# Routing attention and a PReLU feed-forward block on one core: cluster masks on two row tiles, denominators on four column tiles, two weight conversions a step, and v loaded apart from q and k

## The chip, the core and the metric

The kernel runs on one core of one Trainium2 chip. Its metric is the device time of the whole program in microseconds (us). The core's engines are named as in the profile: PE is the matrix engine (PEld its weight loads), DVE the vector engine, ACT the scalar engine, POOL the gpsimd engine, SP the engine whose queue issues nearly all DMAs. Each engine takes its instructions in program order; they wait for one another through semaphores.

## The reference, cut to what matters

```python
# q, k, v: (4, 8, 768, 64); centroids: (8, 16, 64)
q_n, k_n, c_n = (a / (norm(a) + 1e-06) for a in (q, k, centroids))
q_assign = argmax(einsum('bhsd,hcd->bhsc', q_n, c_n), -1)     # the cluster of each query
k_assign = argmax(einsum('bhsd,hcd->bhsc', k_n, c_n), -1)     # the cluster of each key
mask   = q_assign[:, :, :, None] == k_assign[:, :, None, :]
scores = where(mask, q @ k.T / sqrt(64), -1e9)
attn   = exp(scores - max(scores)); attn /= attn.sum(-1) + 1e-09
x      = (attn @ v), heads side by side: (3072, 512)
# w_in: (512, 2048), w_out: (2048, 512), alpha: (2048,), in float64
h = x @ w_in
out = (maximum(h, 0) + alpha * minimum(h, 0)) @ w_out
```

A query attends only to keys of its own cluster. The feed-forward weights arrive as 64-bit floats and are turned into 32-bit ones on the chip.

## The kernel before, in words

**Units of work.** A pair `n` is one batch and two heads: 16 pairs, of which `n < NCH` (0 to 3) are batch 0. The 768 queries of a pair are done in two halves of `HS` = 384. The 768 keys are six chunks of 128, numbered 0 to 5. Scores are held transposed, 128 keys by 384 queries. The order is batch, half, pair; one (batch, half) is a block, and after each block its 384 rows go through the feed-forward part (FFN), in pieces that are fed between the attention steps of the next block: `hidden(f)` (16 of them, one 128-row slice of `h` each, line 614 and its activations) and `final` (lines 634 to 642).

**Steps.** Up to `TOGETHER` (step 24) a step `u` does two chunks (`GROUP`), so a (pair, half) takes three steps. Steps 0 to 11 are block 0 (batch 0, first half, no FFN yet), steps 12 to 23 block 1 (batch 0, second half, with the FFN of block 0). Three or four steps before step 0 load and prepare. From step 24 on a (pair, half) does all six chunks at its first step. In a step the program issues: `score` of this step's chunks; `weigh` of the chunks of the step before; the bookkeeping on DVE; then three slots, each with FFN pieces, preparation of later pairs and weight conversions. `tick()` releases work that was put off by some slots with `later`.

**`score`** does the score matmuls of two chunks (line 461). For batch 0 (`early_mask`) the cluster mask is added in PSUM by four more matmuls per step (line 471): 32 rows of the tile `member` (one-hot clusters of the keys) against 32 rows of `aq` (one-hot clusters of the queries). The keys' one-hot rows of chunk `c` lie in row group `g = (6 + c) // 3`: chunks 0, 1, 2 in rows 64 to 95, chunks 3, 4, 5 in rows 96 to 127. A step takes chunks (0,1), (2,3) or (4,5). ACT then writes `E = exp` (line 482). `prep_queries` fills `aq` one step ahead, for batch 0 by two DVE copies per (pair, half) (line 421). For later batches DVE masks `E` itself (line 495).

**`weigh`** multiplies `E` with `v` into the one PSUM tile `pos` (line 570). In block 0 it also makes the softmax denominators on PE: ones against `E`, 64 output columns for each head (line 565), into `first_den`. When all six chunks are in, DVE transposes `first_den`, takes reciprocals, transposes back to `rd` (lines 576 to 584), and `normalise` (line 591) writes `xT` and frees `pos`. From step 12 on the denominators are sums on DVE: `add_up` (line 508), `turn` (514), `rows_sums` (520), and then `total`, a matmul on PE (line 530), and `invert` (lines 540 to 547). From step 24 on the masks, sums, `total` and `invert` stand in a list `todo`, one entry a slot.

**Preparation.** For pairs of batch 0 `prep_features` transposes q and k on PE in three groups (line 311) into two PSUM buffers in turn, and ACT moves each group to `qkT` (line 315), so the third group waits for the first move. Then comes `square` on ACT (line 323), which frees the raw q and k tiles; `prep_sims` (line 348) and `prep_argmax` (lines 356 to 381) make `member` on DVE. Four pairs of raw tiles would need eight buffers; there are four, so loads wait for `square` of the pair two before.

**Weight conversions.** There are 32, each of 128 x 512 weights. `convert` issues a 512 KB DMA into one of five `raw` tiles (line 230) and at once DVE's `split` (lines 235, 237), which waits for it; four slots later `scale` on ACT (lines 241, 243); two slots later `join` on DVE (lines 247, 250) and on POOL (line 253). In block 0 a step starts one conversion, every fourth step two; in block 1 one and two by turns. The FFN of block 0 needs them in order: `hidden(12)` the first 28, the last `final` all 32. `convert_up_to` forces whatever is missing.

**Loads.** `load(n)` issues on SP's queue the q and k DMAs (line 114; for later batches eight with 128-byte runs, line 119) and then one of v into `vt` (line 125). There are four `vt` buffers, so the v of pair 4 waits until `weigh` has read that of pair 0 for the last time.

```python
        if half == 0:
            load_at.setdefault(max(u - (7 if n < NCH else 9), -AHEAD), []).append(n)
...
        converting = 0 if u < 0 else 1 + (u % 4 == 3) if u < UB else 1 + u % 2
```

Of the kernel before, what the change touches and what calls it, by code (L numbers as in the profile page):

```python
# [14 lines left out]
ALU = mybir.AluOpType  # L15
AX = mybir.AxisListType
PS = bass.MemoryType.PSUM
P = 128
# [3 lines left out]
def kernel(  # L22
# [82 lines left out]
    def load(n):  # L105


        b, hp = pairs[n]
        for w, src in enumerate((q, k)):
            raw = inp.tile([P, NJ, 2, D], FP32, name="qk")  # L110
            for h in range(2):
                rows = src[b, 2 * hp + h]
                if n < NCH:
                    nc.sync.dma_start(out=raw[:, :, h, :],
                                      in_=rows.rearrange("(j p) d -> p j d", p=P))
                    continue
                for x in range(D // Q):
                    r = h * D + x * Q
                    nc.sync.dma_start(
                        out=raw.rearrange("p j h d -> p (j h d)")[r:r + Q, :].rearrange(  # L120
                            "p (t i) -> p t i", i=Q),
                        in_=rows[:, x * Q:(x + 1) * Q].rearrange("(t p) i -> p t i", p=Q))
            raw_qk[n, w] = raw
        vt = vpool.tile([P, 2, NJ, D], FP32, name="vt")
        nc.sync.dma_start(
            out=vt.rearrange("p h j d -> p (h j) d"),
            in_=v[b, 2 * hp:2 * hp + 2].rearrange("h (j p) d -> p (h j) d", p=P))
        vts[n] = vt
# [5 lines left out]
    load(0)  # L134
    load(1)


    ident = const.tile([P, P], FP32, name="ident")
# [291 lines left out]
    assert NJ % GROUP == 0  # L430
# [16 lines left out]
    def score(n, half, chunks, alone=None):  # L447


        qkT = qkTs[n]  # L450
        pss = [[ps_f.tile([P, 512], FP32, name="fps") for h in range(2)] if c == alone else
               ps_s.tile([P, 2, 512], FP32, name="sps") for c in chunks]
        early_mask = n < NCH

        def bank(ps, h):
            return (ps[h] if isinstance(ps, list) else ps[:, h, :])[:, 0:HS]

        for c, ps in zip(chunks, pss):
            for h in range(2):
                r = h * D  # L460
                nc.tensor.matmul(  # L461
                    out=bank(ps, h),
                    lhsT=qkT[r:r + D, S + c * P:S + (c + 1) * P],
                    rhs=qkT[r:r + D, half * HS:(half + 1) * HS], start=True,
                    stop=not early_mask)
        if early_mask:
            for c, ps in zip(chunks, pss):
                g, i = divmod(NJ + c, GT)
                r = slice(g * Q, (g + 1) * Q)
                for h in range(2):  # L470
                    nc.tensor.matmul(  # L471
                        out=bank(ps, h), lhsT=members[n][r, h, i * P:(i + 1) * P],
                        rhs=aqs[n, half][r, 0, :], start=False, stop=True)
        for c, ps in zip(chunks, pss):
            E = e_tiles[0]
            e_tiles.append(e_tiles.pop(0))
            if c == alone:
                for h in range(2):
                    nc.scalar.activation(out=E[:, h, :], in_=ps[h][:, 0:HS], func=AF.Exp,  # L479
                                         scale=SCALE)  # L480
            else:
                nc.scalar.activation(out=E, in_=ps[:, :, 0:HS], func=AF.Exp, scale=SCALE)  # L482
            waiting.append((n, half, c, E))

    def last(m):

        return waiting[len(waiting) - m:]
# [12 lines left out]
    def add_up(chunk, former):  # L500

        n, half, c, E = chunk
        if c == 0:
            return
        if c == 1:
            accs[n, half] = accp.tile([P, 2, HS], FP32, name="acc")
        acc = accs[n, half]
        nc.vector.tensor_tensor(out=acc, in0=former[3] if c == 1 else acc, in1=E,  # L508
                                op=ALU.add)

    def turn(n, half):
# [40 lines left out]
    def weigh(m, denominators=False):  # L552


        first = waiting[:m]
        del waiting[:m]
        n, half, c0, _ = first[0]
        if c0 == 0:
            pos[n, half] = ps_v.tile([P, 512], FP32, name="vps")
        po = pos[n, half]  # L560
        if denominators:
            for _, _, c, e in first:
                for h in range(2):
                    r = h * D
                    nc.tensor.matmul(out=first_den[r:r + D, 0:HS], lhsT=ones,  # L565
                                     rhs=e[:, h, :], start=(c == 0), stop=(c == NJ - 1))
        for _, _, c, e in first:
            for h in range(2):
                r = h * D
                nc.tensor.matmul(out=po[r:r + D, 0:HS], lhsT=vts[n][:, h, c, :],  # L570
                                 rhs=e[:, h, :], start=(c == 0), stop=(c == NJ - 1))
        if denominators and c0 + m == NJ:
# [7 lines left out]
            i = 2 * n + half  # L580
            nc.vector.tensor_reduce(out=lowest[:, i:i + 1], in_=denT[:, :, 0],
                                    axis=AX.X, op=ALU.min)
# [88 lines left out]
    for (n, half), u in start_of.items():  # L671
        def at(step, slot, piece):
            prep_at.setdefault((step, slot), []).append(piece)
        if half == 0:
            load_at.setdefault(max(u - (7 if n < NCH else 9), -AHEAD), []).append(n)
            if n < NCH:
                for g in range(len(groups)):
                    at(u - 4, FIRST + g, lambda n=n, g=g: prep_features(n, g))
# [22 lines left out]
        ffn.extend(ffn_pieces(pairs[n][0], half))  # L701

    for u in range(-AHEAD, TOGETHER):
        for n in load_at.get(u, []):
            if n > 1:
                load(n)
# [14 lines left out]
        if ended:  # L721
            normalise(*prior[:2])
        if u >= UB:
            add_up(last(1)[0], last(2)[0]) if s == 0 else [
                add_up(chunk, None) for chunk in last(GROUP)]
            if s == SB - 1:
                turn(n, half)
                rows_sums(n, half)
# [17 lines left out]
    more_room()  # L746
    todo = deque()
    for u in range(TOGETHER, NS + 1):
        for n in load_at.get(u, []):
            load(n)  # L750
        if u < NS:
            n, half, s = steps[u]
        if s == 0 or u == NS:
# [22 lines left out]
            for c in range(1, NJ):  # L776
                todo.append(lambda c=c, E=E: add_up(E[c], E[c - 1]))
# [7 lines left out]
        for i in slots:  # L785
# [185 lines left out]
```

## Time and profile before

| | |
|---|---|
| Time before | 1036.49 us, median of 4 runs (1035.48 to 1038.55) |
| The profiled execution | 1038.5 us, its span on the core 1036.6 us |
| Busy share of the span | PE 97%, PEld 48%, DVE 65%, ACT 33%, POOL 5% |
| Chain that ended last, by engine | PE 86%, DVE 8%, ACT 2%, DMA 2% |
| Block 0 (step 0 to step 12) | 12.9 to 76.9 us |
| Block 1 (step 12 to step 24) | 76.9 to 215.9 us |
| From step 24 | 215.9 to 1036.6 us |

Times are counted from the start of the span. A record of a 32-bit float matmul on PE is half of one instruction, and the records of different tiles of the array can run side by side; the durations that the profile gives for PE's records overlap, so the text counts from the start of one group to the start of the next. The granted clock (PEclk) is the share of the full PE clock that the throttle let through. The share of busy time is a mean over blocks with different limits, so the blocks are read apart.

### The profile page before, as it was taken

Reading aid. Unit: us, or ns where it says so; the run is one execution under the profiler, and the core shown is the slowest. Engines: PE = TensorE matmul, PEld = TensorE weight load, DVE = VectorE, ACT = ScalarE, POOL = GpSimd, SP = SyncE. Lnnn points to the kernel's source line nnn. Section 1 sums busy time; section 2 is a strip of 40 time slices with the busy share of each in tenths; the row PEclk is TensorE's granted clock in tenths of the full one; section 3 lists DMA queues with packets and bytes.
Section 4 is the critical chain, followed back from the end, with each engine's and each line's share of the span. In section 5 each row is a group of like instructions: output and inputs, shape, how many; then the busy total and the mean of one; then the engine's idle time right before and its main releaser. Section 6 shows DMA issues by size and latency. Waiting matters only on the chain.

```text
span 1036.6 us, 10221 instructions
## 1 busy us (share of the span) xinstructions
PE 1008.4 (97%) x3827; PEld 493.9 (48%) x3827; DVE 673.9 (65%) x1155; ACT 345.5 (33%) x676; POOL 55.7 (5%) x71
## 2 busy tenths in 40 slices
PE   8999999779999999999999999999999999999997
PEld 4444444334454454545455454545445454544553
DVE  4896798767666566868756676768757675663111
ACT  5664444423132233314333142323323141321220
POOL 1332222210000000000000000000000000000000
PEclk9999999989999999999999999999999999999999
DMA  9543543130000230213000212313000000000000
GB/s 220 175 136 71 140 118 63 52 66 10 1 1 11 51 46 19 28 35 57 1 1 0 62 21 26 46 31 62 1 0 1 31 1 0 1 11 20 1 1 33
DMA packets 120936, 42.72 MB, mean 41 GB/s; under 512 B 113696, under 2 KB 113712, under 8 KB 120880
## 3 DMA queue, kind: packets, MB, share of 16 engines
q1 hardware_dynamic: 120704, 41.95, 18.5%
q8 instruction: 32, 0.52, 0.2%
q14 instruction: 24, 0.20, 0.1%
q10 hardware_dynamic: 176, 0.04, 0.0%
HBM read 35.69 MB, written 6.29 MB: 41 GB/s over the span
## 4 chain that ended last, share of the span: by engine, by line
PE 86%; DVE 8%; ACT 2%; DMA 2%; issue 1%; SPq 1%; POOL 1%; DVEq 0%; POOLq 0%; ACTq 0%
PE fps L634 31%; PE fps L614 28%; PE vps L570 11%; PE sps L461 9%; PE fps L461 4%; DVE acc L508 2%; PE sps L471 1%; PE fps L565 1%; PE mps L348 1%; DVE gT L606 1%; DVE acc L514 1%; DMA raw<-in_moe_w_in_dram 1%; DVE qkT L330 1%; DVE part L520 1%; DMA raw<-in_moe_w_out_dram 1%
## 5 line engine op out<-in xcount | busy, mean ns | idle before, releaser
L614 PE MATMUL fps<-xT,w_in_sb 128*128 128x384 f32 x1024 | 343.2, 492 | 3.4 <-POOL w_in_sb L253 3.4
L634 PE MATMUL fps<-w_out_sb,gT 128*128 128x512 f32 x768 | 337.1, 595 | 7.2 <-POOL w_out_sb L253 7.0
L614 PEld LDWEIGHTS fps<-xT,w_in_sb 128*128 128x128 f32 x1024 | 192.0, 191 | 147.9 <-issue 7.0
L634 PEld LDWEIGHTS fps<-w_out_sb,gT 128*128 128x128 f32 x768 | 144.7, 190 | 184.9 <-issue 165.9
L606 DVE SCALAR_TENSOR_TENSOR gT<-neg,alpha_neg,gT 128x384 f32<-128x384 f32 x128 | 86.4, 677 | 156.1 <-ACT neg L622 155.5
L621 ACT ACTIVATE gT<-fps 128x384 f32<-128x384 f32 x128 | 62.9, 491 | 276.1 <-PE fps L614 276.1
L461 PE MATMUL sps<-qkT 64*128 64x384 f32 x576 | 112.4, 509 | 0.0
L495 DVE SCALAR_TENSOR_TENSOR raw<-aq,key,raw 128x384 f32<-128x384 bf16 x160 | 88.6, 613 | 15.5 <-ACT raw L482 9.8
L482 ACT ACTIVATE E<-sps 128x768 f32<-128x768 f32 x88 | 67.2, 813 | 72.7 <-PE sps L471 46.3
L570 PE MATMUL vps<-E,vt 128*64 128x384 f32 x448 | 81.6, 491 | 0.0
L495 DVE SCALAR_TENSOR_TENSOR E<-aq,key,E 128x384 f32<-128x384 bf16 x128 | 70.9, 612 | 10.3 <-ACT E L482 6.8
L461 PEld LDWEIGHTS sps<-qkT 64*128 64x128 f32 x576 | 52.6, 190 | 41.2 <-issue 9.9
L508 DVE TENSOR_TENSOR acc<-acc,E 128x768 f32<-128x768 f32 x64 | 61.5, 960 | 15.5 <-ACT E L482 13.3
L642 DVE TENSOR_TENSOR y<-y,fps 128x512 f32<-128x512 f32 x30 | 20.6, 685 | 67.5 <-PE fps L634 67.5
L482 ACT ACTIVATE raw<-sps 128x768 f32<-128x768 f32 x56 | 43.0, 814 | 60.4 <-PE sps L461 60.0
L622 ACT ACTIVATE neg<-fps 128x384 f32<-128x384 f32 x128 | 62.0, 484 | 0.6 <-DVE gT L606 0.6
L640 ACT COPY y<-fps 128x512 f32<-128x512 f32 x24 | 14.1, 586 | 131.9 <-PE fps L634 131.9
L570 PE MATMUL vps<-raw,vt 128*64 128x384 f32 x320 | 56.5, 491 | 0.0
L570 PEld LDWEIGHTS vps<-E,vt 128*64 128x64 f32 x448 | 30.5, 137 | 41.9 <-issue 41.4
L508 DVE TENSOR_TENSOR acc<-acc,raw 128x768 f32<-128x768 f32 x48 | 45.9, 956 | 1.2
L461 PE MATMUL fps<-qkT 64*128 64x384 f32 x192 | 42.1, 516 | 0.0
L479 ACT ACTIVATE raw<-fps 128x384 f32<-128x384 f32 x48 | 21.0, 492 | 48.5 <-PE fps L461 48.5
(100 smaller groups left out, 655.8 us busy)
## 6 DMA issues: line engine op xcount, KB each, us to landing
raw<-in_moe_w_in_dram SPq DMA_DIRECT2D x16, 512.0 KB, 4.7
raw<-in_moe_w_out_dram SPq DMA_DIRECT2D x16, 512.0 KB, 6.0
vt<-in_v_dram SPq DMA_DIRECT2D x16, 384.0 KB, 4.4
out_dram<-y SPq DMA_DIRECT2D x24, 256.0 KB, 2.0
qk<-in_q_dram SPq DMA_DIRECT2D x48, 96.0 KB, 3.9
qk<-in_k_dram SPq DMA_DIRECT2D x48, 96.0 KB, 3.7
qk<-in_q_dram SPq DMA_DIRECT2D x8, 192.0 KB, 4.8
qk<-in_k_dram SPq DMA_DIRECT2D x8, 192.0 KB, 4.5
```

Source lines behind the costliest of these rows:

```text
L461: nc.tensor.matmul(out=bank(ps, h), lhsT=qkT[r:r + D, S + c * P:S + (c + 1) * P], rhs=qkT[r:r + D, half * HS:(half + 1) * HS], start=True, ...
L479: nc.scalar.activation(out=E[:, h, :], in_=ps[h][:, 0:HS], func=AF.Exp, scale=SCALE)
L482: nc.scalar.activation(out=E, in_=ps[:, :, 0:HS], func=AF.Exp, scale=SCALE)
L495: nc.vector.scalar_tensor_tensor(out=E[:, h, :], in0=aqs[n, half][:, h, :], scalar=keys[n][:, NJ + c, h:h + 1], in1=E[:, h, :], op0=ALU.is ...
L508: nc.vector.tensor_tensor(out=acc, in0=former[3] if c == 1 else acc, in1=E, op=ALU.add)
L570: nc.tensor.matmul(out=po[r:r + D, 0:HS], lhsT=vts[n][:, h, c, :], rhs=e[:, h, :], start=(c == 0), stop=(c == NJ - 1))
L606: nc.vector.scalar_tensor_tensor(out=gs[f], in0=neg, scalar=alpha_neg[:, f:f + 1], in1=gs[f], op0=ALU.mult, op1=ALU.add)
L614: nc.tensor.matmul(out=ps[:, 0:HS], lhsT=w_in_sb[:, c, f * P:(f + 1) * P], rhs=xT[:, c, :], start=(c == 0), stop=(c == NCH - 1))
L621: nc.scalar.activation(out=gs[f], in_=ps[:, 0:HS], func=AF.Relu)
L622: nc.scalar.activation(out=neg, in_=ps[:, 0:HS], func=AF.Relu, scale=-1.0)
L634: nc.tensor.matmul(out=ps[:, 0:DM], lhsT=gs[f][:, i * P:(i + 1) * P], rhs=w_out_sb[:, f, :], start=on and f == f0, stop=off and f == f0 + ...
L642: nc.vector.tensor_tensor(out=ys[i], in0=ys[i], in1=ps[:, 0:DM], op=ALU.add)
```

## The change

It has five parts. The chunks of a step become (0,3), (1,4), (2,5), and the mask matmuls go head by head over the two chunks, so that two that follow each other use different row groups. The denominators are made on four column tiles of 32, each with half of the queries (192), so eight matmuls of half the length stand where four stood; DVE's transposition of `first_den` is half as long, and four small reciprocals and two small copies stand where one reciprocal stood. The copies that fill `aq` for batch 0 go from DVE to ACT. In block 1 every step starts two conversions. For later batches v is issued two steps after q and k. In the list from step 24 on, `turn` and `rows_sums` share one slot, an empty entry stands ahead of `total`, and each slot's entry is issued ahead of its FFN pieces. `add_up` takes the first two chunks of a (pair, half) in whatever order they come.

```diff
+    def load_v(n):
+        b, hp = pairs[n]
         vt = vpool.tile([P, 2, NJ, D], FP32, name="vt")
         nc.sync.dma_start(
...
                 for g in range(NG // 2, NG):
-                    nc.vector.tensor_copy(out=aqs[n, half][g * Q:(g + 1) * Q, 0, :],
-                                          in_=members[n][r, 0, :])
+                    nc.scalar.copy(aqs[n, half][g * Q:(g + 1) * Q, 0, :],
+                                   members[n][r, 0, :])
...
         if early_mask:
-            for c, ps in zip(chunks, pss):
-                g, i = divmod(NJ + c, GT)
-                r = slice(g * Q, (g + 1) * Q)
-                for h in range(2):
+            for h in range(2):
+                for c, ps in zip(chunks, pss):
+                    g, i = divmod(NJ + c, GT)
+                    r = slice(g * Q, (g + 1) * Q)
                     nc.tensor.matmul(
                         out=bank(ps, h), lhsT=members[n][r, h, i * P:(i + 1) * P],
                         rhs=aqs[n, half][r, 0, :], start=False, stop=True)
...
             for _, _, c, e in first:
                 for h in range(2):
-                    r = h * D
-                    nc.tensor.matmul(out=first_den[r:r + D, 0:HS], lhsT=ones,
-                                     rhs=e[:, h, :], start=(c == 0), stop=(c == NJ - 1))
+                    for x in range(2):
+                        r = h * D + x * Q
+                        nc.tensor.matmul(out=first_den[r:r + Q, 0:HS // 2],
+                                         lhsT=ones[:, 0:Q],
+                                         rhs=e[:, h, x * HS // 2:(x + 1) * HS // 2],
+                                         start=(c == 0), stop=(c == NJ - 1))
...
-            nc.vector.transpose(out=denT.rearrange("p x i -> p (x i)"),
-                                in_=first_den[:, 0:HS])
+            nc.vector.transpose(
+                out=denT[:, 0:NX // 2, :].rearrange("p x i -> p (x i)"),
+                in_=first_den[:, 0:HS // 2])
...
             inv = rdp.tile([P, 2 * NX], FP32, name="inv")
-            nc.vector.reciprocal(out=inv[:, 0:NX], in_=denT[:, :, 0])
+            for g in range(P // Q):
+                h, x = divmod(g, 2)
+                nc.vector.reciprocal(
+                    out=inv[h * D:h * D + Q, x * NX // 2:(x + 1) * NX // 2],
+                    in_=denT[g * Q:(g + 1) * Q, 0:NX // 2, 0])
+            for h in range(2):
+                nc.vector.tensor_copy(out=inv[h * D + Q:(h + 1) * D, 0:NX],
+                                      in_=inv[h * D:h * D + Q, 0:NX])
...
-            load_at.setdefault(max(u - (7 if n < NCH else 9), -AHEAD), []).append(n)
+            if n < NCH:
+                load_at.setdefault(max(u - 7, -AHEAD), []).append(
+                    lambda n=n: n < 2 or (load(n), load_v(n)))
+            else:
+                load_at.setdefault(u - 9, []).append(lambda n=n: load(n))
+                load_at.setdefault(u - 7, []).append(lambda n=n: load_v(n))
...
-            score(n, half, range(s * GROUP, (s + 1) * GROUP))
+            score(n, half, range(s, NJ, SB))
...
-        converting = 0 if u < 0 else 1 + (u % 4 == 3) if u < UB else 1 + u % 2
+        converting = 0 if u < 0 else 1 + (u % 4 == 3) if u < UB else 2
...
-            todo.append(lambda n=n, half=half: turn(n, half))
-            todo.append(lambda n=n, half=half: rows_sums(n, half))
+            todo.append(lambda n=n, half=half: (turn(n, half), rows_sums(n, half)))
+            todo.append(lambda: None)
             todo.append(lambda n=n, half=half: total(n, half))
...
+            todo.popleft()()
             feed(max(pieces, 0))
             if (s, i) == (SB - 1, SLOTS - 1) and unfinished[0]:
                 feed(1)
             if s > 0:
                 prepare(u, i)
-            todo.popleft()()
```

More of the change, by code (lines that the diff above doesn't have):

```diff
@@ L133 @@
     nc.scalar.dma_start(out=alf, in_=moe_alpha.rearrange("(f p) -> f p", p=P))
-    load(0)
-    load(1)
+    for n in range(2):
+        load(n)
+        load_v(n)
     ident = const.tile([P, P], FP32, name="ident")
@@ L429 @@
     SB = NJ // GROUP
-    assert NJ % GROUP == 0
+    assert NJ == GROUP * SB and SB == GT
     steps = [(b * NCH + hp, half, s)
@@ L498, in mask, with add_up @@
                 in1=E[:, h, :], op0=ALU.is_equal, op1=ALU.mult)
-    def add_up(chunk, former):
+    def add_up(chunk, first=None):
         n, half, c, E = chunk
-        if c == 0:
-            return
-        if c == 1:
+        if first is not None:
             accs[n, half] = accp.tile([P, 2, HS], FP32, name="acc")
         acc = accs[n, half]
-        nc.vector.tensor_tensor(out=acc, in0=former[3] if c == 1 else acc, in1=E,
+        nc.vector.tensor_tensor(out=acc, in0=acc if first is None else first[3], in1=E,
                                 op=ALU.add)
@@ L556, in weigh @@
         del waiting[:m]
-        n, half, c0, _ = first[0]
-        if c0 == 0:
+        n, half = first[0][:2]
+        done = first[-1][2] == NJ - 1
+        if (n, half) not in pos:
             pos[n, half] = ps_v.tile([P, 512], FP32, name="vps")
@@ L571, in weigh @@
                                  rhs=e[:, h, :], start=(c == 0), stop=(c == NJ - 1))
-        if denominators and c0 + m == NJ:
+        if denominators and done:
             denT = asg.tile([P, NX, Q], FP32, name="simT")
-            nc.vector.transpose(out=denT.rearrange("p x i -> p (x i)"),
-                                in_=first_den[:, 0:HS])
-            inv = rdp.tile([P, 2 * NX], FP32, name="inv")
-            nc.vector.reciprocal(out=inv[:, 0:NX], in_=denT[:, :, 0])
-            i = 2 * n + half
-            nc.vector.tensor_reduce(out=lowest[:, i:i + 1], in_=denT[:, :, 0],
-                                    axis=AX.X, op=ALU.min)
+            nc.vector.transpose(
+                out=denT[:, 0:NX // 2, :].rearrange("p x i -> p (x i)"),
+                in_=first_den[:, 0:HS // 2])
+            i = 2 * n + half
+            nc.vector.tensor_reduce(out=lowest[:, i:i + 1], in_=denT[:, 0:NX // 2, 0],
+                                    axis=AX.X, op=ALU.min)
+            inv = rdp.tile([P, 2 * NX], FP32, name="inv")
+            for g in range(P // Q):
[6 more added lines that the diff above has]
+                                      in_=inv[h * D:h * D + Q, 0:NX])
             rd = rdp.tile([P, HS], FP32, name="rd")
@@ L703 @@
     for u in range(-AHEAD, TOGETHER):
-        for n in load_at.get(u, []):
-            if n > 1:
-                load(n)
+        for piece in load_at.get(u, []):
+            piece()
         n, half, s = steps[max(u, 0)]
@@ L723 @@
         if u >= UB:
-            add_up(last(1)[0], last(2)[0]) if s == 0 else [
-                add_up(chunk, None) for chunk in last(GROUP)]
+            if s == 0:
+                add_up(last(1)[0], last(2)[0])
+            else:
+                for chunk in last(GROUP):
+                    add_up(chunk)
             if s == SB - 1:
@@ L748 @@
     for u in range(TOGETHER, NS + 1):
-        for n in load_at.get(u, []):
-            load(n)
+        for piece in load_at.get(u, []):
+            piece()
         if u < NS:
@@ L775 @@
                 todo.append(lambda c=c, E=E: mask(E[c]))
-            for c in range(1, NJ):
-                todo.append(lambda c=c, E=E: add_up(E[c], E[c - 1]))
-            todo.append(lambda n=n, half=half: turn(n, half))
-            todo.append(lambda n=n, half=half: rows_sums(n, half))
+            todo.append(lambda E=E: add_up(E[1], E[0]))
+            for c in range(2, NJ):
+                todo.append(lambda c=c, E=E: add_up(E[c]))
+            todo.append(lambda n=n, half=half: (turn(n, half), rows_sums(n, half)))
+            todo.append(lambda: None)
             todo.append(lambda n=n, half=half: total(n, half))
```

## The prediction

> **What bounds the kernel now.** I read the windows by block first, because the page's 97% for PE is a mean.
>
> ```profile
> 12.90:46.88 33.98, 31.45 (x193) 13.76 (x193) 27.00 (x56) 22.60 (x39) 6.55 (x5) 1.00 0.77 205
> 46.88:76.86 29.98, 29.98 (x177) 12.04 (x176) 28.34 (x54) 19.19 (x31) 12.27 (x8) 1.00 0.46 140
> 76.86:139.31 62.45, 62.26 (x239) 28.96 (x237) 47.20 (x73) 28.06 (x49) 14.81 (x9) 1.00 0.43 93
> 182.56:215.92 33.36, 22.94 (x82) 10.27 (x81) 25.10 (x41) 11.27 (x21) 8.43 (x5) 0.86 0.07 27
> 215.92:251.50 35.58, 33.50 (x113) 16.94 (x112) 26.15 (x47) 10.81 (x23) 0.00 (x0) 0.89 0.29 56
> 251.50:947.00 695.50, 692.38 (x2578) 342.66 (x2578) 467.26 (x784) 211.03 (x429) 0.00 (x0) 1.00 0.11 21
> ```
>
> The columns are the stretch, PE, PEld, DVE, ACT, POOL, the granted clock, DMA share and GB/s. From 251 us to 947 PE has nothing to give back but 3.1 us. The loss is at 182 to 251 us: PE idle for 12.5 us and throttled besides. In the second half of block 0 DVE is as full (28.34 of 29.98) as PE, which will matter. Next, who ended PE's waits, from the waits of PE:
>
> ```profile
> PE fps L634 <- POOL w_out_sb L253: 7.0, 2, 3.6
> PE mps L530 <- DVE part L520: 5.2, 7, 2.1
> PE fps L614 <- POOL w_in_sb L253: 3.4, 1, 3.4
> PE fps L311 <- ACT qkT L315: 1.6, 3, 1.1
> ```
>
> So three waits of 10.4 us for the last converted weights, and seven for `total`. Behind the weights, from the waits of DVE and then of SP's queue:
>
> ```profile
> DVE power L235 <- DMA raw<-in_moe_w_in_dram: 12.0, 4, 5.1
> DVE power L235 <- DMA raw<-in_moe_w_out_dram: 4.1, 1, 4.1
> ```
>
> ```profile
> SPq L125 <- PE vps L570: 203.8, 11, 27.2
> ```
>
> The v load holds SP's queue until `weigh` frees its buffer, the weight DMAs queue behind it, and DVE stands still for them: 5.1, 1.0 and 4.1 us of these waits are in block 1.
>
> What the waits cost beyond themselves, from the windows over the throttled stretches:
>
> ```profile
> 186.23:189.64 3.41, 3.41 (x10) 1.18 (x9) 2.25 (x6) 0.87 (x2) 0.00 (x0) 0.50 0.03 7
> 210.12:220.36 10.24, 6.70 (x18) 3.34 (x20) 5.96 (x14) 1.82 (x3) 1.26 (x1) 0.50 0.29 60
> 247.67:251.08 3.41, 3.41 (x7) 1.67 (x5) 2.59 (x8) 0.00 (x0) 0.00 (x0) 0.50 0.00 0
> ```
>
> Each follows a wait of 2.1 to 3.6 us; each halves the clock (0.50).
>
> **Masks.** From the timeline of PE in block 0:
>
> ```profile
> 63.76 0.82 PE L471 MATMUL sps<-aq,member 32*128 32x384 bf16 x4
> 64.51 1.51 PE L565 MATMUL fps<-E,ones 128*64 128x384 f32 x8
> 65.85 1.46 PE L570 MATMUL vps<-E,vt 128*64 128x384 f32 x8
> 67.24 1.56 PE L461 MATMUL sps<-qkT 64*128 64x384 f32 x8
> 68.73 0.50 PE L471 MATMUL sps<-aq,member 32*128 32x384 bf16 x4
> 69.16 1.51 PE L565 MATMUL fps<-E,ones 128*64 128x384 f32 x8
> ```
>
> Start to start, the four masks take 0.75 us for chunks (4,5), (0,1) alike, one row group, and 0.43 for (2,3), which straddles two groups. After the change all do: 16 steps x 0.32 = 5.1 us of PE, 2.6 in each block.
>
> **Denominators.** Now 1.34 us a step (64.51 to 65.85). The new form, sixteen records of 192 columns on four column tiles, is not in the trace; nearest is the `prep_sims` group (line 348), eight records of 384 columns on four tiles, which with its switches of tile shape takes 0.78 (16.42 to 17.20). Same columns, so 0.78 to 0.85, taken 0.80: 12 steps x 0.54 = 6.5 us. Ends: 0 gained if the tiles go in pairs, 7.7 if the four rounds take the 0.16 each that half of a 0.32 round gives with nothing else. The new shape may add a switch a step; the row for one is line 570, four rounds that start 0.32 apart in a slot of 1.39 (65.85 to 67.24), so 0.11, and twelve more would lose 1.3 us. [...]
>
> DVE's end of a half (lines 576 to 584) took 1.5 us; half a transposition less (0.3), five small operations more (0.12 to 0.15 each, rows of lines 579 and 581) makes 2.0.
>
> **Block 0 does not get this 9.1 us (6.5 + 2.6).** The `aq` copies now stand in ACT's queue, ahead of the moves of the next pair's features (line 315).
> At the start: those moves began at 11.12 us; now they wait behind two copies that wait for `member`'s transposition (line 378, done 14.51). No such ACT copy is in the trace; 0.24 (line 397, 96 columns) and 0.47 (line 315, 512 columns, start to start) bound it, taken 0.39. So the first move starts at 15.3, PE's third group at 16.0 instead of 12.37, and PE idles 3.6 us, as long as the waits that halved the clock. Step 0's mask no longer waits 1.2. Step 1 starts at 19.2 to 20.7 instead of 17.20. Behind it on ACT is `square` of pair 1, which frees the tiles for which SP's queue waits (18.56), and behind that the weight DMA issued at 23.76, which ended DVE's wait at 30.78. I put that landing 2.2 us later (1.5 to 3.5).
> From there DVE had work without a gap to 49.86, with ACT behind it:
>
> ```profile
> 42.00 0.72 ACT L241 ACTIVATE power<-power,low_exp 128x512 uint32<-128x512 uint32 x1 [2.77 <-DVE power L235]
> 45.66 0.58 ACT L315 COPY qkT<-fps 128x512 f32<-128x512 f32 x1
> ```
>
> 42.00 becomes 44.7 (2.2, and 0.5 for DVE's longer end). The move comes 3.66 later plus 0.78 of copies: 49.1. Step 6 starts at 50.3, not 46.88: 3.4 late. PE will have idled some 5 us before it, at half clock after (1.7).
> Steps 6 to 12: step 6 saves 0.86. Then PE's 30.0 us between the ends of the denominators in steps 6 and 12 shrink by 6 x 0.54 + 4 x 0.32 to 25.5, but DVE's 17.2 us without a gap (50.68 to 67.91) shrink only to 16.2 (1.5 of copies at 62.20 off, 0.5 on) where PE wants 13.1. DVE ends 3.1 late, `normalise` frees `pos` 1.8 late for step 10. So 27.3.
> Sum: 3.4 + 1.7 - 0.9 - 2.7 = +1.5 us, later than now. With the landing unmoved and no throttling, -3; with 3.5 and longer throttling, +5.
>
> **Block 1.** All 32 conversions are issued by step 20 (15 in block 0, 18 in nine steps); now 28, the number that `hidden(12)` in step 21 needs. The v loads no longer wait: pair 4's comes at step 17, pair 0 was read in step 15. So the three waits go: 10.4 us, and the throttled work in them (half of 3.41, and of 213.66 to 215.92): 2.8. The masks give 2.6. DVE is the cover: in steps 12 to 20 (76.86 to 172.46, 95.6 us) it is busy 76.7; four more conversions cost 1.9 each by their four start-to-starts (0.34, 0.34, 0.60, 0.60), and 1.0 for the stretching of DVE's records while POOL works (line 237 takes 1.51 at 78.53, else 0.42); less 2 for `aq`. 86 of 93 us, and 10.2 us of waits for DMAs gone. It will be late after steps 17 and 20, which hold `qkT` transpositions, by 5 to 7 us, against `total`'s cover (`part` done 106.7, `total` at 110.44: 3.7). I take 2.0 of new waits (0 to 6). ACT's added copies, 2 x 0.39 every third step, lie in its idle time (28.06 of 62.45). Sum: -13.8.
>
> **Step 24 on.** The clock was still half to 220.36 (2.2 lost); `total` waited 2.1 at 244.67 and throttled 3.41 us (1.7). `rows_sums` now stands two FFN pieces ahead of `total` rather than one, and the sums ahead of the pieces they waited behind: 6.0, taken 5.7. [...] The other six waits for `part`, 3.1: taken 3.0. SP's later waits for v hold nothing that PE waits for.
>
> **Sum.** +1.5 - 13.8 - 5.7 - 3.0 = -21.0, a span of 1015.6 against 1036.6. The profiled execution took 1038.5, 2.0 above the median; the difference taken off both gives 1017.5 and 1015.5. I say 1016.
>
> **Rivals.**
> *Block 0 takes its gain*: ACT's copies are not held up, DVE keeps pace, block 0 gives 9.1 instead of +1.5: 1005. For it, DVE waited for the denominators twice (0.8, 0.6 us at 49.9 and 80.0); against it, ACT's order.
> *The weights stay late*: five `raw` buffers, and the eight short-run q and k DMAs ahead of the weights on SP's queue (six us of issue at 150.9) still starve DVE, and the three waits and their throttling (10.4 + 2.8 + 2.2) stay: with the 2.0 of new waits out, 1029.5. For it, SP waited 64 us for `raw` tiles; against, every conversion is earlier.
> *Slower*: DVE becomes the bound of steps 12 to 20. If its demand passes 98 us instead of 86 it is late by more than 3.7 us in every step; PE idles 2 us a step and, as at 247.67, loses 1.7 to the clock: 9 x 3.7 = 33, less the 2.0 counted: 1047.
>
> **How the numbers follow.** Forecast 0.67, block 0's gain 0.14, late weights 0.11, slower 0.08. The forecast's own ends (block 0 -3 to +5, waits 0 to 6, `total` unchanged 3) give 1009 to 1027; the range takes in the first two rivals: 1004 to 1030. A measurement of this kernel can tell about 0.3%, 3 us, from no change: faster 0.90, within 0.02 (late weights with a worse block 0), slower 0.08.
>
> **What would show it.** Right: masks 0.43 in every step, line 565's successor near 0.8, no wait for POOL, SP's waits for PE near nothing, no wait for `part` over 1 us; a PE wait for `qkT` of 3 to 5 us near 12 and 45 us; step 12 starting near 78. Wrong: step 12 near 68 (block 0 gained), a clock of 0.5 in 140 to 215, or PE waiting there for DVE.

## The result, and the profile after

The changed kernel takes 1034.43 us, the median of 51 runs (1032.79 to 1036.49), against 1035.83 us for 78 runs of the kernel before (1032.57 to 1040.84). The ratio is 0.9986, 95% interval 0.998 to 0.9991: by the bound of 0.3% no difference that counts, where 1016 was forecast. The profiled spans are 1031.9 and 1036.6 us. They differ by 4.7 and not by 1.4 because the profiled execution of before lay 2.7 above the median of its 78 runs and that of after 0.8 below the median of its 51; the traces are compared span against span.

The windows over the stretches of the profile after. The columns are the stretch, PE, PEld, DVE, ACT, POOL, granted clock, DMA share and GB/s. The stretches are step 0 to step 6, step 6 to step 12, the group that starts at step 24, and the rest up to the same point of the end as before:

```profile
17.62:53.27 35.65, 29.83 (x233) 12.89 (x233) 24.00 (x53) 24.38 (x42) 7.32 (x5) 0.93 0.60 183
53.27:83.97 30.70, 28.60 (x226) 11.34 (x225) 25.86 (x57) 19.87 (x33) 9.97 (x7) 0.91 0.36 107
207.80:238.42 30.62, 29.61 (x111) 15.25 (x110) 26.52 (x48) 10.57 (x23) 0.00 (x0) 1.00 0.31 65
238.42:942.40 703.98, 695.92 (x2579) 340.53 (x2578) 471.11 (x785) 210.89 (x429) 0.00 (x0) 1.00 0.11 21
```

Step 0 begins 4.7 us later and step 12 at 83.97 in place of 76.86: block 0 is 7.1 us longer, and its clock fell below 1.00 in both halves. Block 1 (83.97 to 207.80) takes 123.83 in place of 139.06, 15.2 less. The group of step 24 takes 30.62 in place of 35.49, 4.9 less. The last line is where the most was lost: it takes 703.98 us where before took 695.50, though the work on PE is the same. To the end of the span this part is 8.25 us longer. So 7.1 - 15.2 - 4.9 + 8.25 = -4.7.

The waits of PE name who gave it back:

```profile
PE fps L315 <- ACT qkT L319: 9.7, 3, 4.5
PE mps L532 <- ACT every L401: 7.1, 10, 1.0
PE sps L475 <- ACT aq L425: 2.1, 2, 1.9
PE mps L532 <- DVE part L522: 2.0, 7, 0.3
```

The columns are total, times and longest; `fps`, `mps`, `sps` and `vps` are tiles in PSUM. The three waits for POOL are gone. In their place stand 9.7 us for the moves of the features (1.6 before), 2.1 for `aq`, which was not foreseen, and ten waits of `total` (line 532) for `every`, ACT's cast of another pair's clusters, which was not foreseen either.

The two edits on PE did per step what they were meant to. From the timeline of PE in step 7:

```profile
60.66 0.50 PE L475 MATMUL sps<-aq,member 32*128 32x384 bf16 x4
61.08 0.86 PE L570 MATMUL fps<-E,ones 128*32 128x192 f32 x16
61.87 1.51 PE L577 MATMUL vps<-E,vt 128*64 128x384 f32 x8
```

Start to start the four masks take 0.42 (0.75 before, for two thirds of the steps) and the denominators 0.79 (1.34 before). A step of block 0 without waits takes 4.15 us in place of 4.66 or 4.97. Yet the block became longer.

### The profile page after: what moved, and what is told of

Same layout as the page of the kernel before. It is cut to its first block, busy times and chain, and to the rows that moved or that the text cites. A ratio compares the mean times of both kernels' runs of the same rounds, so it can differ in the third digit from the quotient of the medians.

```text
span 1031.9 us, 10431 instructions
## 1 busy us (share of the span) xinstructions
PE 1000.4 (97%) x3923; PEld 487.4 (47%) x3923; DVE 667.3 (65%) x1159; ACT 354.1 (34%) x692; POOL 50.4 (5%) x71
## 4 chain that ended last, share of the span: by engine, by line
PE 86%; DVE 7%; ACT 3%; DMA 1%; issue 1%; SPq 1%; POOL 0%; DVEq 0%; POOLq 0%; ACTq 0%
PE fps L649 30%; PE fps L629 29%; PE vps L577 11%; PE sps L465 8%; PE fps L465 3%; DVE acc L510 2%; DMA raw<-in_moe_w_in_dram 1%; PE mps L352 1%; DVE acc L516 1%; PE mps L532 1%; DVE gT L621 1%; DVE part L522 1%; PE sps L475 1%; DVE power L251 1%; ACT E L486 1%
## 5 line engine op out<-in xcount | busy, mean ns | idle before, releaser
L621 DVE SCALAR_TENSOR_TENSOR gT<-neg,alpha_neg,gT 128x384 f32<-128x384 f32 x128 | 81.1, 636 | 125.9 <-ACT neg L637 124.4
L499 DVE SCALAR_TENSOR_TENSOR raw<-aq,key,raw 128x384 f32<-128x384 bf16 x160 | 88.8, 613 | 37.8 <-ACT raw L486 26.3
L499 DVE SCALAR_TENSOR_TENSOR E<-aq,key,E 128x384 f32<-128x384 bf16 x128 | 71.3, 612 | 17.9 <-ACT E L486 12.2
```

The costliest lines, as they stand in the source:

```text
L499: nc.vector.scalar_tensor_tensor(out=E[:, h, :], in0=aqs[n, half][:, h, :], scalar=keys[n][:, NJ + c, h:h + 1], in1=E[:, h, :], op0=ALU.is ...
L621: nc.vector.scalar_tensor_tensor(out=gs[f], in0=neg, scalar=alpha_neg[:, f:f + 1], in1=gs[f], op0=ALU.mult, op1=ALU.add)
```

## The experiments

Twelve kernels ran, in three sets of four. Each set has its own runs of the kernel before; their medians were 1037.09, 1035.86 and 1036.25. The changed kernel's 51 runs belong to none of them, but to the 78 of the kernel before. Differences are given between medians; across sets the ratios can put them up to 1.7 us elsewhere, and where that matters both are given. "Rest" is from the second group after step 24 (step 27) to the end of the span. "Piece" is short for `total` behind its FFN piece.

| kernel | step 12 at | step 24 at | rest | median us | ratio to before, 95% |
|---|---|---|---|---|---|
| before | 76.86 | 215.92 | 785.2 | 1035.83 | |
| changed | 83.97 | 207.80 | 793.5 | 1034.43 | 0.998 to 0.9991 |
| changed, `aq` on DVE | 79.95 | 205.92 | 793.8 | 1030.88 | 0.9918 to 0.9957 |
| changed, old late order | 82.97 | 207.58 | 785.1 | 1027.51 | 0.9888 to 0.9926 |
| changed, piece | 83.30 | 207.90 | 780.6 | 1021.04 | 0.9831 to 0.9875 |
| piece, `aq` on DVE | 77.89 | 203.84 | 780.4 | 1016.54 | 0.978 to 0.982 |
| piece, `aq` on DVE, 12 conversions | 75.38 | 202.51 | 780.4 | 1009.95 | 0.9729 to 0.9767 |
| piece, `aq` on DVE, old denominators | 75.32 | 200.54 | 780.5 | 1013.94 | 0.9771 to 0.981 |
| the same with 12 conversions | 75.42 | 201.35 | 780.4 | 1014.19 | 0.9767 to 0.9795 |
| piece, `aq` on ACT behind moves | 79.25 | 203.25 | 780.4 | 1015.80 | 0.9784 to 0.9814 |
| the same, 12 conversions | 70.24 | 194.92 | 780.7 | 1008.15 | 0.9715 to 0.9741 |
| the same, 12 conversions, old denominators | 73.95 | 198.95 | 780.4 | 1012.10 | 0.9751 to 0.9777 |
| before, v apart | 76.71 | 210.47 | 785.1 | 1032.76 | 0.9949 to 0.9982 |
| before, two conversions | 76.91 | 208.20 | 785.5 | 1027.94 | 0.9907 to 0.9942 |

The starts of steps come from one profiled execution each. Block 0 scatters: of kernels that are alike up to step 24, the changed one and the two that differ from it only in the late order differ by up to 1.0 us at step 12, and the two with 15 conversions, new denominators and `aq` on DVE by 2.1. For "piece, `aq` on DVE, 12 conversions" the profiled execution (1015.3) was the longest of its six runs, so its steps are not used below.

### The late sums

**The old order of the late steps.** This undoes the last edit of "The change", which speaks of five parts and lists six. Each entry of `todo` is taken behind the FFN piece and the preparation of its slot again, and `turn` and `rows_sums` take two entries.

```
-            todo.popleft()()
             feed(max(pieces, 0))
...
             if s > 0:
                 prepare(u, i)
+            todo.popleft()()
```

> The changed kernel with the old order of the late steps: each step's piece of the sums behind the FFN piece and the preparation of its slot, turn and rows_sums in two slots. Theory (total ahead of its FFN piece costs the 8.25 us from step 27 on): the 28-us and 27-us groups are back at 28.1 and 26.7, PE waits for `every` vanish, two waits of 1.15 us for part come back; step 24's group grows from 30.6 to 33 to 34.5 as total waits 2.1 us and throttles again: 4 to 6 us shorter, 1029 to 1031. Rival (the extra time comes from elsewhere: from ACT, from SP's later v loads or from the split load): groups stay 0.6 to 0.8 us longer each, and with step 24's group longer the whole is 2 to 4 us longer, 1037 to 1039.

Measured 1027.51, 6.9 shorter than the changed kernel, where 4 to 6 were forecast; the profiled span is 5.9 shorter. The rest is 785.1, as in the kernel before, and the group of step 24 takes 33.36. So the whole of the 8.25 us comes from the new order.

**`total` alone behind its piece.** All else of the new order stays.

```
+            totalling = (s, i) == (SB - 1, SLOTS - 2)
+            if not totalling:
+                todo.popleft()()
             feed(max(pieces, 0))
+            if totalling:
+                todo.popleft()()
```

> The changed kernel, its new order of the sums kept, except that total stands behind the FFN piece of its slot again. Theory (the loss is total's place, ahead of a piece, where it waits for ACT's every to leave the one mps buffer and for part): no PE wait for every, none for part over 0.3 us, step 24's group stays at 30.6 to 31, every later group is as long as in the kernel before or 1.4 shorter; from step 27 on 2 to 3 us less than before in place of 8.25 more: 10 to 12 us shorter, 1022 to 1024.5. Rival (the early row sums hold up DVE's other work, masks and slopes, and so PE): the groups stay 0.6 to 0.8 longer, 1033 to 1035.

Measured 1021.04, 13.4 shorter. The rest is 780.6: 12.9 less than in the changed kernel, and 4.6 less than in the kernel before, where the theory had 2 to 3. No wait for `part` is left, and one for `every`, of 1.0 in the group of step 24. PE's timeline at the end of the same (pair, half) shows it, first in the changed kernel:

```profile
417.34 0.25 PE L397 MATMUL mps<-first,spread 128*128 128x24 bf16 x4
418.59 0.40 PE L532 MATMUL mps<-part,fold 128*128 128x24 f32 x2 [1.00 <-ACT every L401]
418.84 2.83 PE L629 MATMUL fps<-xT,w_in_sb 128*128 128x384 f32 x8
```

and with `total` behind its piece:

```profile
415.69 0.25 PE L397 MATMUL mps<-first,spread 128*128 128x24 bf16 x4
415.80 2.83 PE L629 MATMUL fps<-xT,w_in_sb 128*128 128x384 f32 x8
418.46 0.30 PE L532 MATMUL mps<-part,fold 128*128 128x24 f32 x2
```

Both matmul groups write `mps`. `prep_clusters` (line 397) fills that buffer at the end of the slot before, and `total` needs it again at the start of the next slot. It is free only after ACT's cast. With the FFN piece between the two the cast is hidden; without it PE stands, 1.00 us here. The rival, that early row sums hold up DVE, falls: they stay early here.

### Block 0

**The `aq` copies back on DVE.**

```
-                    nc.scalar.copy(aqs[n, half][g * Q:(g + 1) * Q, 0, :],
-                                   members[n][r, 0, :])
+                    nc.vector.tensor_copy(out=aqs[n, half][g * Q:(g + 1) * Q, 0, :],
+                                          in_=members[n][r, 0, :])
```

> The changed kernel with the aq copies of pairs 0 to 3 back on DVE, nothing else. Theory (ACT's order eats block 0's gain): PE's waits for qkT of 4.0 us (at 12.6) and 4.5 us (at 47.7) shrink to those of the kernel before, 0.2 and 1.2, the half clock at 14.3, 51.8 and 72.3 us goes, the first raw tile lands near 31 us again, step 12 starts at 68 to 72 us in place of 83.97, and the whole is 12 to 16 us shorter: 1019 to 1022. Rival (DVE was as full as PE in block 0 and can't take the copies back): DVE ends late instead, PE waits for DVE's member, split or denominators in its place, step 12 starts at 76 us or later, and the whole is at most 8 us shorter: 1027 or more.

Measured 1030.88, 3.6 shorter than the changed kernel, and step 12 at 79.95: the rival. The start is healed (step 1 at 17.25), the second raw tile is there at 31.07 (30.78 in the kernel before, 34.75 in the changed one), but PE's wait for `qkT` in step 5 is still 4.2 us, and the mean granted clock of this execution is 0.996 (0.993 in the changed kernel). ACT's timeline shows what holds the move:

```profile
43.05 0.72 ACT L245 ACTIVATE power<-power,low_exp 128x512 uint32<-128x512 uint32 x1 [4.54 <-DVE power L239]
43.68 0.61 ACT L247 ACTIVATE w_out_sb<-w_out_sb 128x512 f32<-128x512 uint32 x1
44.20 1.49 ACT L486 ACTIVATE E<-sps 128x768 f32<-128x768 f32 x2
45.58 0.72 ACT L245 ACTIVATE power<-power,low_exp 128x512 uint32<-128x512 uint32 x1
46.20 0.62 ACT L247 ACTIVATE w_out_sb<-w_out_sb 128x512 f32<-128x512 uint32 x1
46.72 0.58 ACT L319 COPY qkT<-fps 128x512 f32<-128x512 f32 x1
```

ACT stands 4.5 us at a conversion's `scale`, which waits for DVE's `split`; the exponentials and the move are queued behind. DVE works without a gap from 31.07 to 50.91. The move comes at 46.72 where it came at 45.66 in the kernel before: DVE began 0.3 later there, and its end of a half takes 2.4 us (32.95 to `normalise` at 35.34) in place of 1.5. PE, which is quicker now, comes to this point earlier and only waits longer.

**Both.** `total` behind its piece, and `aq` on DVE.

> The changed kernel with the aq copies back on DVE and total behind its FFN piece. Theory (the two losses are apart in time and add): the two savings sum, 22 to 28 us shorter than the changed kernel: 1007 to 1012. Rival (DVE can't take the copies): only total's saving and a little, 1018 to 1024.

Measured 1016.54, 4.5 shorter than with `total` alone. Between the two forecasts, nearer to the rival. The two savings do add, as the theory had it: 3.6 and 13.4 against 17.9 together. Its 22 to 28 had counted on the 12 to 16 that `aq` on DVE did not give.

**One conversion a step in block 0**, 12 of the 32 in place of 15, on top of both.

```
-        converting = 0 if u < 0 else 1 + (u % 4 == 3) if u < UB else 2
+        converting = 0 if u < 0 else 1 if u < UB else 2
```

> The kernel with the aq copies on DVE and total behind its FFN piece (1016.54), with one conversion a step in block 0 in place of one and at times two: 12 in block 0 and not 15. Theory (block 0 is bound by DVE, without a gap from 31 to 51 us, with ACT's scale behind it and the moves of the features behind that): three conversions less, each 2.0 us of DVE and 1.3 of ACT, bring the move of step 5 from 46.7 to 43 to 44.5, PE's wait there from 4.2 us to under 2, without half clock after; step 12 starts at 71 to 75 in place of 78 to 80; block 1 takes the three on without a wait for POOL: 5 to 8 us shorter, 1008 to 1012. Rival (block 0 is bound by when the raw tiles land, not by how much DVE has to do): step 12 stays at 77 or later, and the whole is at 1015 to 1018. Rival (block 1 can't take them): PE waits for w_out_sb or w_in_sb before 205 us, 1018 or more.

Measured 1009.95, 6.6 shorter (5.4 by the ratios), with no wait of PE for a weight anywhere. The 20 conversions in block 1 are not quite free: in its profiled execution PE's wait for `lowest`, a small DVE operation there, is 2.2 us where it was 1.5 without this edit, and the mean granted clock is 0.994 where it was 0.997. The time is as the theory had it; its profiled execution can't show the step.

**The old denominators**, on top of both: two column tiles of 384 columns, and DVE's old end of a half.

```
-                    for x in range(2):
-                        r = h * D + x * Q
-                        nc.tensor.matmul(out=first_den[r:r + Q, 0:HS // 2],
...
+                    r = h * D
+                    nc.tensor.matmul(out=first_den[r:r + D, 0:HS], lhsT=ones,
+                                     rhs=e[:, h, :], start=(c == 0), stop=(c == NJ - 1))
```

> The kernel with the aq copies on DVE and total behind its FFN piece (1016.54), with the old denominators: two column tiles of 384 columns, 1.34 us a step of PE in place of 0.79, and DVE's end of a half with one transposition and one reciprocal, 1.0 us shorter. Theory (block 0 is bound by DVE and ACT, so PE's 6.5 us there turn into waits and half clock): step 12 starts at 76.5 to 79, no later than with the new ones, and the whole is within 2 us of 1016.5 or shorter. Rival (the new denominators give what they take off PE, and the rest of block 0's loss is something else): step 12 at 82 to 86, 4 to 6.5 us longer, 1020.5 to 1023.

Measured 1013.94, 2.6 shorter than with the new ones by the medians, 0.9 by the ratios, whose intervals overlap: no difference is shown. So 6.5 us of PE's work were given back, and the time did not rise. The windows of this kernel from step 0 to 6 and from 6 to 12:

```profile
12.90:46.32 33.42, 30.54 (x193) 13.04 (x193) 27.04 (x56) 22.48 (x39) 6.53 (x5) 1.00 0.77 208
46.32:75.32 29.00, 29.00 (x178) 11.39 (x177) 27.71 (x52) 19.13 (x31) 10.77 (x8) 1.00 0.41 132
```

PE is full in the second half and the clock is 1.00 throughout; DVE, busy 27.7 of 29.0, has little room to be faster than that. With 15 conversions the new denominators do not shorten block 0. The edit also takes some 0.8 us off DVE at each of four ends of a half, and no run parts this from PE's share.

**The old denominators with 12 conversions.**

> The kernel with the aq copies on DVE, total behind its piece and one conversion a step in block 0 (1009.95), with the old denominators. Theory (once DVE has room, PE bounds block 0 and the new denominators are worth something): 2 to 5 us longer than with the new ones, 1012 to 1015, where at 15 conversions they cost 2.6. Rival (DVE and ACT bound block 0 still, and PE's saving is lost to waits and half clock whatever is converted): the old ones are 1 to 3 us shorter here too, 1007 to 1009.

Measured 1014.19: 4.2 longer than with the new ones, 3.4 by the ratios. With DVE relieved the new denominators are worth something.

**`aq` on ACT, behind two moves**: the copies two slots later, on top of the kernel with `total` behind its piece.

```
-            at(u - 1, FIRST + h, lambda n=n, half=half, h=h: prep_queries(n, half, h))
+            at(u - 1, FIRST + (2 if n < NCH else h),
+               lambda n=n, half=half, h=h: prep_queries(n, half, h))
```

> The kernel with total behind its FFN piece and the aq copies on ACT (1021.04), with these copies put off by two slots: behind the first two moves of the next pair's features on ACT's queue, in place of ahead of all three. Theory (what costs is the order, not ACT): PE's waits for qkT fall from 9.2 us to under 5, the first move is back at 11 us and the first step's mask waits 1 to 2 us for aq instead; step 12 starts at 75 to 80 in place of 83.3, 3 to 6 us shorter: 1015 to 1018, as with the copies on DVE or better. Rival (ACT is too full in block 0 wherever the copies stand): step 12 at 82 or later, 1020 to 1022.

Measured 1015.80, 5.2 shorter than with the copies ahead of the moves. So it is their place in ACT's queue that cost, not their being on ACT. In step 5 PE still waits 3.6 us for `qkT`, and 2.7 us for `aq` in step 9: with 15 conversions the chain through DVE remains.

**The same with 12 conversions, with the new and the old denominators.**

> The aq copies on ACT behind two moves, total behind its piece, one conversion a step in block 0, new denominators: every loss found so far taken out with the change's parts all kept. Theory (block 0's bound is the sum of what DVE and ACT do ahead of the moves): DVE is rid of 2.4 us of copies each half as well, step 12 at 71 to 75, 1004 to 1009. Rival (DVE is no longer the bound after the conversions are fewer): no better than with the copies on DVE, 1009 to 1012.

> The same with the old denominators. Theory (with DVE and ACT rid of work, PE bounds block 0): 3 to 6 us longer than with the new ones. Rival (the half clock after a wait takes what the new ones save): the same within 1.5 us, or shorter.

Measured 1008.15 and 1012.10. The new denominators are worth 4.0 us here. The first is the best kernel of the study, 0.9728 of before (0.9715 to 0.9741). Its windows from step 0 to 6 and 6 to 12:

```profile
12.71:43.95 31.24, 28.06 (x233) 12.30 (x232) 23.33 (x54) 23.66 (x42) 4.59 (x4) 1.00 0.79 210
43.95:70.24 26.29, 26.05 (x225) 10.54 (x225) 23.15 (x53) 19.51 (x33) 11.43 (x7) 1.00 0.43 130
```

In the second half DVE is busy 23.2 of 26.3 us (28.3 of 30.0 in the kernel before), PE waits 0.2 us, the clock is 1.00 in both, and step 12 starts 6.6 us earlier than in the kernel before.

### Block 1

**v apart alone, and two conversions alone**, each on the kernel before.

> The kernel before, with v loaded apart from q and k, nothing else. Theory (the v load that holds SP's queue, with the weights behind it, is what makes block 1's weights late): SP's wait for vps falls from 204 to about 118 us, the three waits of PE for w_in_sb and w_out_sb go from 10.4 us to under 3, and so does most of the half clock there: 8 to 13 us shorter, 1024 to 1029. Rival (too few conversions a step is what makes them late): the waits stay at 7 us or more, at most 4 us shorter.

> The kernel before, with two conversions a step in block 1, nothing else. Theory (the held queue is the cause, and more conversions only queue up behind it): the waits for w_in_sb and w_out_sb stay at 6 us or more, 0 to 5 us shorter, 1032 to 1037. Rival (the count is the cause): the waits go, 9 to 13 us shorter, 1024 to 1028.

Measured 1032.76 (3.1 shorter) and 1027.94 (7.9 shorter). The waits went as the rival has it in both cases; the gain of the second is somewhat under its 9 to 13. In that kernel PE has new waits for DVE, 3.0 us for `gT` and 2.6 for `lowest`. With v apart two of the three waits stay, though SP's queue waits for `vps` 118 us in place of 204. The line from the waits of PE of that kernel:

```profile
PE fps L638 <- POOL w_out_sb L257: 7.0, 2, 3.6
```

With two conversions a step and v where it was, no wait for POOL is left and the clock is 1.00 from 182.56 to 215.92 us (0.86 in the kernel before), though SP's queue still stands for v. From the waits of SP's queue of that kernel:

```profile
SPq L125 <- PE vps L570: 182.3, 11, 27.3
```

So it was the number of conversions that made the weights late, and the held queue in a smaller part: v apart leaves the two waits for `w_out_sb` and takes away the one for `w_in_sb`. Block 1 is 131.3 us with two conversions, 133.8 with v apart and 123.8 with both and the masks, against 139.1.

## Why the prediction was wrong, step by step

The span was forecast at 1015.6 and came to 1031.9. The 16.3 us are 5.6 in block 0, -1.4 in block 1, 0.8 in the group of step 24, and 11.25 in the rest.

**The step that failed most is "the other six waits for `part`, 3.1: taken 3.0".** It looked at the one producer that the waits of PE named, `part`, and not at the other thing that `total` needs, a free `mps` buffer. The order changed for both: the row sums came earlier, but `total` itself was pulled ahead of the FFN piece that had hidden ACT's cast. Nor did two pieces cover `part`: in DVE's timeline the sums stand behind slopes (line 621) of earlier pieces, of which the one at 353.25 had stood 1.96 us for `neg`, which ACT makes of PE's `fps`, so that `part` was done 0.05 us before `total` began at 357.78. Ten waits for `every` came, five of them of 1.0 us, and seven of 0.2 to 0.3 for `part`; each costs more than its gap (last section). Measured +8.25. With `total` left behind its piece the same edit gives -4.6, more than the 3.0: two waits of 1.15 for `part` had cost 1.4 each, and four of 0.20 had cost 0.45 each.

**Block 0, +1.5, came to +7.1.** The mechanism was the one forecast, ACT's copies ahead of the moves; its terms were too small. Two copies take 1.03 us, not 0.78; one takes 0.51, beyond the 0.24 to 0.47 that were to bound it. The first wait is 4.0, not 3.6, 6.8 us of half clock follow, and step 1 starts at 22.17, past the 19.2 to 20.7. From ACT's timeline of the changed kernel, then PE's, then the window:

```profile
14.88 1.03 ACT L425 COPY aq<-member 32x384 bf16<-32x384 bf16 x2 [4.41 <-DVE member L382]
15.93 0.59 ACT L319 COPY qkT<-fps 128x512 f32<-128x512 f32 x1
16.57 1.11 PE L315 MATMUL fps<-ident,qk 128*128 128x128 f32 x4 [4.00 <-ACT qkT L319]
14.29:21.11 6.82, 4.54 (x16) 2.03 (x16) 1.56 (x4) 2.68 (x5) 0.00 (x0) 0.50 1.17 272
```

The raw tile lands 4.0 us later, not 2.2, as DVE's timeline of the changed kernel shows:

```profile
34.75 0.43 DVE L239 TENSOR_SCALAR power<-raw 128x512 uint32<-128x512 uint32 x1 [5.84 <-DMA raw<-in_moe_w_in_dram]
```

With that the move of step 5 stands at 51.59, not 49.1, and step 6 begins at 53.27, not 50.3. Not foreseen at all was step 9: there the copies are queued behind a `scale` that waits for DVE's `split`, the mask waits 2.1 us for `aq`, and 3.4 us of half clock follow. The forecast listed DVE's queue as the limit of this half and then let only `normalise` be late.

What the forecast did not say is the larger point: even without ACT's order, 9.1 us less on PE would have given little here. With `aq` on DVE step 12 came at 79.95 and 77.89, and with the copies behind the moves at 79.25, no earlier than before. The rival "block 0 takes its gain" needed two more things, 12 conversions and the copies behind the moves; with both, DVE kept pace and block 0 gave 6.6 of the rival's 9.1 us. That 1008.15 is so near its 1005 is in part luck: the late sums gave 4.5 in that kernel, not the 3.0 counted on.

**Block 1, -13.8, came to -15.2.** Masks 2.6 and no waits for POOL, as said; of the 2.0 us of new waits 1.5 came. The count of conversions, 28 issued by step 20, carried it, as the experiments show; the text before it, which put the lateness on v's hold of SP's queue, named the smaller cause. The sum came out near because the change held both edits.

**Step 24, -5.7, came to -4.9.** The half clock and the wait of 2.1 for `part` went; a wait of 1.0 for `every` came.

**The per-step prices** of masks (0.43, measured 0.42) and denominators (0.80, measured 0.79) held. Of the 0.11 a step allowed for a switch of tile shape, an estimate of the author's, 0.05 came: line 577 behind the new denominators takes 1.44 (61.87 to 63.31), its like before 1.39. That the switch is what takes it was not shown. The upper end of the gain was added up wrong: four rounds of 0.16 leave 0.70 a step, 8.4 us and not 7.7; no other figure rests on it. DVE's end of a half was put at 2.0 us and takes 2.4 (from 74.71 to `normalise` at 77.07 in the changed kernel).

**The rivals.** Late weights did not come: PE waits for no converted weight. DVE as the bound of block 1 did not come either: the new waits there are 1.5 us. The class that came, no difference, had been given 0.02, because no case was made for the sums of the last 700 us being worse than before. They had been taken as a gain or nothing.

## What to carry to other kernels

When an instruction is moved ahead of other work on its engine, list all that it waits for: each operand and the buffer it writes. The profile of before named one of them, `part` (5.2 us in seven waits), and the work that is jumped over may have hidden the others. Work taken off the busiest engine shortens a stage only where the others have room: in block 0 the same edit (the new denominators) was worth nothing that shows or 4 us, by whether three conversions had been taken off DVE and ACT. A wait is passed on to what stands behind it in the same queue: ahead of a move that PE waits for, two copies of 0.5 us each for every pair, with their own wait for DVE (4.41 us for the first pair), cost the kernel 3.6 to 5.2 us.

## What the runs showed of the hardware

**The granted clock changed at points whole multiples of 3.41 us apart.** Up to 960 us it changes in the kernel before at 186.23, 189.64, 210.12, 220.36, 247.67 and 251.08 us, and in the changed kernel at 14.29, 21.11, 51.83, 55.25, 72.31 and 75.73. Adding up PE's idle time in each stretch of 3.41 us that these points mark off: of the stretches at full clock, the three in each trace with 2.0 us or more of idle (3.12, 2.28 and 2.08; 2.02, 3.42 and 2.10) were followed by half clock, and none of the others, with 1.2 us at most. The same wait can be cheap or dear: 2.1 us for `part` left the clock alone in "before, two conversions", where the mean granted clock was 0.999, at most 3.1 us of half clock in its span of 1025.4, and the same wait at 244.67 in the kernel before was followed by 3.41 us at 0.50. That it depends on where the wait falls among such stretches is the author's reading.

**A wait cost more than its gap.** Records of PE overlapped: in the lines with `total` behind its piece, the one at 415.80 lasts 2.83, and the next group begins 2.66 later. So the gap that the profile shows there would begin some 0.17 us late, by the author's estimate. The groups with a gap of 1.00 for `every` are 1.27 us longer than without it (28.92 and 27.65), those with 0.32 for `part` 0.68 (27.36 and 26.68). Of this 0.09 is `total` standing ahead of a piece without any wait (31.89 and 31.80). Together this makes up the 1.27; of the 0.68, 0.10 stays unexplained.

**The `aq` copy took longer on ACT.** The 32 x 384 bf16 copy takes 0.51 us on ACT (changed kernel, 16 copies) and 0.25 on DVE (median of 16); but some of DVE's take 1.2, as in the kernel before.
